# List products of the first four units, six pipeline steps later in the program

## The chip, the cores and the metric

One Trainium2 chip, one of its cores. The metric is the device time of one execution in microseconds (us). Before the change it is 1176.56 us, the median of 3 runs (1169.21 to 1182.27).

## What is computed

A depthwise causal convolution of seven taps over 8 x 2880 tokens of 192 channels, then a mixture of experts with one expert of 16 for each token. The reference, cut to what matters:

```python
out = np.einsum('hk,bskhg->bshg', softmax(weight), x_unf)      # 8 heads, 7 taps
x = out.reshape(23040, 192)
g_idx = np.argmax(x @ w_group, axis=1)                         # 4 groups
for g in range(4):
    xg = x[g_idx == g]
    e_idx = np.argmax(xg @ w_expert[g], axis=1)                # 4 experts of the group
    for e in range(4):
        h = np.maximum(xg[e_idx == e] @ w1[g, e], 0.0)         # 192 -> 1024
        out[tokens] = (g_w * e_w)[:, None] * (h @ w2[g, e])    # 1024 -> 192
```

## The kernel before

The 23040 tokens are cut into 192 blocks of 120 tokens, and these into 18 units: unit 0 has 4 blocks, unit 1 has 8, unit 2 has 12, units 3, 4 and 5 have 8, all others 12. `unit(u)` (line 392) is a generator. Each `yield` in it ends a step. Its steps are, in order: the load of the unit's x; eight convolution products, one for each head (line 416), each with its copy out of PSUM on ScalarE (lines 421 and 423); transposes of the result (lines 434 and 445); the router's logits (lines 459 and 464); the routing on VectorE (lines 495 to 524); the write of the convolved rows and gates to a table in memory (`xcd`, lines 425 and 528); the position of each token in its expert's list, from two small products with the running counts (lines 535 and 536) and a chain on VectorE (lines 539 to 572); and last the list product (line 577), which turns two one-hot matrices (`ohl`, line 564, and `ohv`, line 563) into a piece of each expert's token list, which VectorE finishes (lines 580 and 581) and GpSimd scatters into `idtab` (line 583). `finished(u)` then marks the unit as routed.

`step()` advances one live unit by one step, in rotation. Up to four units are live at first (`LIVE1`), and a new one is taken in when the newest has done a set number of steps (`SK`, 8 or 9). The main program calls `step()` until unit 4 is routed (`NEED` is 5). In that loop, at fixed counts of calls (`KPRE`: 40, 100, 112, 120, 126, 138), it also starts the weights of the first two experts and splits those of the first (`weights`, `split_one`, lines 613 to 629). A copy of such a split on ScalarE is pinned to its place in the program's order (`pin`). Then it opens the first two slots: the lists are read back (`open_portion`, line 975, on SP's queue) and the tokens' rows are gathered (`gather`, line 648, on GpSimd's queue). After that it makes another 72 calls (`AHEAD`), and then the expert phase begins: 256 tokens a slot, turned (line 661), hidden layer (line 679), output layer (line 697 and 701), scatter (line 752). The remaining units are spread over the slots at a rate which `stages_to` works out.

The written order is not each engine's order. A planner in the framework orders each engine's queue by when it expects an instruction's inputs; of several that are ready by its reckoning, the one that stands earlier in the program goes first. Once built, each engine takes its own queue in order.

Between the chain on VectorE and the list product stand some empty steps: `LISTLAG`, 8, from unit 5 on, and `LISTLAG0`, none, for units 0 to 4.

Of the kernel before, what the change touches and what calls it, by code (L numbers as in the profile page):

```python
# [35 lines left out]
def conv_moe_kernel(  # L36
# [56 lines left out]
    NEED = 5  # L93
# [12 lines left out]
    QGB = 3  # L106
    AHEAD = 72
    LISTLAG = 8
    LISTLAG0 = 0
    HOLD = 4  # L110
    LAG_S = 1
    HB = 4
# [17 lines left out]
    FRU = 99  # L130
    FRE = nc.gpsimd
    FRH = 0
# [254 lines left out]
    def gaps(u):  # L387

        return tuple(UG[4 * u:4 * u + 4]) if 4 * u < len(UG) else (GA, GL, GB, REST)


    def unit(u, pre=None):
# [177 lines left out]
        nc.vector.tensor_tensor(out=rows[:, 0:E], in0=eo, in1=sel, op=ALU.mult)  # L570
        nc.vector.tensor_reduce(out=rows[:, E:E + 1], in_=rows[:, 0:E], axis=AX.X, op=ALU.add)
        nc.vector.tensor_tensor(out=rowi, in0=rows[:, E:E + 1], in1=goff, op=ALU.add)
        for _ in range(LISTLAG if u >= NEED else LISTLAG0 if u < NEED - 1 else 0):
            yield
        pl = bank("l")
        for b in range(nb):
# [319 lines left out]

    def stages(u):
        q = units[u][1] // QB
        return 1 + 8 + (2 * FRH if u >= FRU else 0) + sum(gaps(u)) + 3 * q + 1 + (LISTLAG if u >= NEED else 0)

    SKEW1 = 8
    LIVE1 = 4
# [4 lines left out]
    def stages_to(n):  # L907
        extra = sum(max(0, stages(n) - i * SKEW2) for i in range(1, LIVE2)) if n < NU else 0
        return sum(stages(u) for u in range(n)) + extra
# [7 lines left out]
    def step():  # L917

        if routed[0] < NU and len(live) < lead[1] and (not live or max(live, key=lambda a: a[0])[1] >= (lead[0] or SK[min(routed[0], len(SK)) - 1])):
            u = routed[0]  # L920
            live.append([u, 0, unit(u, xin0 if u == 0 else None)])
            routed[0] += 1
        if not live:
            return
        done[0] += 1
        cur = live.pop(0)
        cur[1] += 1
        try:
            next(cur[2])
            live.append(cur)  # L930
        except StopIteration:
            pass
# [122 lines left out]
    while routed[1] < portions[0][0]:  # L1055
# [3 lines left out]
        for i in [i for i, kk in enumerate(KPRE) if kk == k]:  # L1059
            e, q = divmod(i, 5)  # L1060
# [162 lines left out]
```

## Time and profile before

| | us |
|---|---|
| median of 3 runs | 1176.56 |
| lowest and highest run | 1169.21, 1182.27 |
| profiled execution, its time | 1175.41 |
| profiled execution, its span | 1173.3 |
| TensorE busy in the span | 1115.3 |
| VectorE busy | 805.5 |
| ScalarE busy | 672.9 |
| first product of the expert phase | 102.85 after the span's start |

The profile is of one execution, whose time lies 2.1 us above its span and 1.15 us under the median. Busy time counts an engine as busy also where TensorE's clock is granted at its lower level, so a stretch can be full and slow at once. The granted clock stands in a column of its own, 1.00 for 2.4 GHz and 0.50 for 1.2 GHz, as a mean over the stretch.

### The profile page before, as it was taken

The numbers are of one execution on the slowest core, as the hardware profiler recorded it, in microseconds if no ns is written. First come the engines' busy times: TensorE is split into PE (matmuls) and PEld (weight loads), VectorE is DVE, ScalarE is ACT, GpSimd is POOL, SyncE is SP. The second block draws the span as 40 slices with busy tenths as digits, with TensorE's granted clock in tenths as the row PEclk, the third lists the DMA queues.
The fourth block names the chain that finished last, engine by engine and source line by source line (L and its number), as shares of the span: only waits on it lengthen the run. The fifth ranks groups of instructions, "written<-read, shape, count | busy, mean of one in ns | idle before, by whom it ended". The sixth has DMA issues, their size and how long they took to land. (4 is left out here: it accounts for less than half of the span.)

```text
span 1173.3 us, 23973 instructions
## 1 busy us (share of the span) xinstructions
PE 1115.3 (95%) x8468; PEld 1082.8 (92%) x8468; DVE 805.5 (69%) x1667; ACT 672.9 (57%) x1326; POOL 480.8 (41%) x432
## 2 busy tenths in 40 slices
PE   6799899999899999999999999999999999999993
PEld 6678899999899999999999999999999999999993
DVE  3757978886777676575678665666676767776671
ACT  4554566665565555646544555555676666766651
POOL 1002422345334343434435444444455655655541
PEclk9887899999899999999999999999999999999997
DMA  7989588979795564436454556444666667766630
GB/s 210 250 171 247 142 221 229 217 195 248 185 235 142 137 171 138 135 102 159 118 151 120 138 86 169 142 130 135 186 176 185 172 192 205 205 175 182 179 96 14
DMA packets 194093, 196.20 MB, mean 167 GB/s; under 512 B 49443, under 2 KB 171181, under 8 KB 193966
## 3 DMA queue, kind: packets, MB, share of 16 engines
q1 hardware_dynamic: 127424, 140.43, 45.0%
q0 software_dynamic: 18528, 36.09, 11.0%
q10 hardware_dynamic: 48014, 18.10, 7.4%
q8 instruction: 67, 1.10, 0.4%
q14 instruction: 60, 0.49, 0.2%
HBM read 159.08 MB, written 36.85 MB: 167 GB/s over the span
## 5 line engine op out<-in xcount | busy, mean ns | idle before, releaser
L697 PE MATMUL po<-cw,hh 128*128 128x384 f32 x1424 | 447.2, 371 | 11.7 <-DVE ys L749 9.4
L679 PE MATMUL ph<-xa,ah 128*128 128x256 f32 x1424 | 389.7, 295 | 0.7 <-DVE xa L664 0.7
L685 DVE SCALAR_TENSOR_TENSOR hl<-ph,hh 128x512 fp32r<-128x512 f32 x356 | 241.5, 686 | 174.0 <-ACT hh L684 173.6
L701 PE MATMUL po<-cw,hl 128*128 128x192 f32 x1424 | 358.3, 252 | 0.6 <-issue 0.3
L752 POOL DMA_INDIRECT out<-ys,idp x160 | 171.3, 1071 | 432.0 <-DVE ys L749 361.2
L684 ACT ACTIVATE hh<-ph 128x512 fp32r<-128x512 f32 x356 | 210.4, 595 | 231.4 <-PE ph L679 210.1
L697 PEld LDWEIGHTS po<-cw,hh 128*128 128x128 f32 x1424 | 269.7, 189 | 17.2 <-DVE ys L749 12.0
L701 PEld LDWEIGHTS po<-cw,hl 128*128 128x128 f32 x1424 | 273.8, 192 | 2.9 <-DVE hl L685 0.5
L679 PEld LDWEIGHTS ph<-xa,ah 128*128 128x128 f32 x1424 | 272.8, 192 | 3.1 <-DVE xa L664 1.0
L648 POOL DMA_INDIRECT xg<-xcd,idp x160 | 182.7, 1142 | 59.8 <-issue 27.1
L679 PE MATMUL ph<-xb,bl 128*128 128x256 f32 x712 | 202.1, 284 | 1.1 <-DVE bl L622 1.1
L679 PE MATMUL ph<-xa,al 128*128 128x256 f32 x712 | 202.2, 284 | 0.0
L679 PE MATMUL ph<-xb,bh 128*128 128x256 f32 x712 | 202.1, 284 | 0.0
L629 DVE TENSOR_TENSOR cw<-raw,cw 128x768 fp32r<-128x768 f32 x132 | 130.9, 1019 | 16.3 <-ACT cw L628 16.1
L679 PEld LDWEIGHTS ph<-xa,al 128*128 128x128 f32 x712 | 137.4, 193 | 1.8
L679 PEld LDWEIGHTS ph<-xb,bl 128*128 128x128 f32 x712 | 137.0, 192 | 1.3 <-DVE bl L622 1.3
L679 PEld LDWEIGHTS ph<-xb,bh 128*128 128x128 f32 x712 | 136.5, 192 | 0.0
L628 ACT ACTIVATE cw<-raw 128x768 fp32r<-128x768 f32 x132 | 105.4, 840 | 0.1
L614 DVE TENSOR_TENSOR al<-raw,ah 128x1024 fp32r<-128x1024 f32 x66 | 81.3, 1232 | 32.7 <-ACT ah L613 31.9
L749 DVE SCALAR_TENSOR_TENSOR ys<-po,xg,ys 128x192 f32<-128x192 f32 x187 | 75.7, 415 | 31.5 <-ACT ys L748 26.6
L667 ACT ACTIVATE xb<-pm 64x256 fp32r<-64x256 f32 (+1 forms) x98 | 36.1, 368 | 105.5 <-DVE xa L664 105.1
L748 ACT ACTIVATE ys<-po,xg 128x192 f32<-128x192 f32 x187 | 75.7, 418 | 28.7 <-PE po L701 14.0
(222 smaller groups left out, 1484.4 us busy)
## 6 DMA issues: line engine op xcount, KB each, us to landing
raw<-in_moe_w SPq DMA_DIRECT2D x132, 384.0 KB
raw<-in_moe_w SPq DMA_DIRECT2D x66, 512.0 KB
raw<-in_moe_w SPq DMA_DIRECT2D x132, 256.0 KB
xcd<-xc ACTq DMA_DIRECT2D x13, 742.5 KB
xin<-in_x SPq DMA_DIRECT2D x7, 1134.0 KB
xin<-in_x SPq DMA_DIRECT2D x6, 1039.5 KB
xcd<-xcb ACTq DMA_DIRECT2D x13, 360.0 KB
xg<-xcd,idp POOLq DMA_INDIRECT x160
```

The costliest lines, as they stand in the source:

```text
L614: eng.get(k, nc.vector).tensor_tensor(out=al, in0=ra, in1=ah.bitcast(F32), op=ALU.subtract)
L628: pin(PINW, nc.scalar.activation(out=cw[:, fs, 0, :], in_=rc[k - 2], func=AF.Copy))
L629: eng.get(k, nc.vector).tensor_tensor(out=cw[:, fs, 1, :], in0=rc[k - 2], in1=cw[:, fs, 0, :].bitcast(F32), op=ALU.subtract,)
L648: nc.gpsimd.indirect_dma_start(out=xs[:, t, :], out_offset=None, in_=xcd[0:known, :], in_offset=bass.IndirectOffsetOnAxis(ap=ids[:, t:t + ...
L679: nc.tensor.matmul(out=hp[:, j], lhsT=wgt[:, fs], rhs=xx, start=i == 0, stop=i == len(ops) - 1)
L684: nc.scalar.activation(out=hh, in_=hp, func=AF.Relu)
L685: nc.vector.scalar_tensor_tensor(out=hl, in0=hp, scalar=0.0, in1=hh.bitcast(F32), op0=ALU.max, op1=ALU.subtract,)
L697: nc.tensor.matmul(out=oo[t][:, 0:2 * D], lhsT=hh[:, j, ts], rhs=cw[:, f].rearrange("p a d -> p (a d)"), start=f == 0, stop=False,)
L701: nc.tensor.matmul(out=oo[t][:, 0:D], lhsT=hl[:, j, ts], rhs=cw[:, f, 0, :], start=False, stop=f == NF - 1,)
L748: nc.scalar.activation(out=ys[:, t, :], in_=oo[t][:, D:2 * D], func=AF.Copy, scale=g)
L749: nc.vector.scalar_tensor_tensor(out=ys[:, t, :], in0=oo[t][:, 0:D], scalar=g, in1=ys[:, t, :], op0=ALU.mult, op1=ALU.add,)
L752: nc.gpsimd.indirect_dma_start(out=outviews[nscat[0] % len(outviews)], out_offset=bass.IndirectOffsetOnAxis(ap=ids[:, t:t + 1].bitcast(U32 ...
```

## The change

```diff
-    LISTLAG0 = 0
+    LISTLAG0 = (6, 6, 6, 6, 0)
...
         nc.vector.tensor_tensor(out=rowi, in0=rows[:, E:E + 1], in1=goff, op=ALU.add)
-        for _ in range(LISTLAG if u >= NEED else LISTLAG0 if u < NEED - 1 else 0):
+        for _ in range(LISTLAG0[u] if u < NEED else LISTLAG):
             yield
         pl = bank("l")
...
     def stages(u):
         q = units[u][1] // QB
-        return 1 + 8 + (2 * FRH if u >= FRU else 0) + sum(gaps(u)) + 3 * q + 1 + (LISTLAG if u >= NEED else 0)
+        return 1 + 8 + (2 * FRH if u >= FRU else 0) + sum(gaps(u)) + 3 * q + 1 + (LISTLAG if u >= NEED else LISTLAG0[u])
```

Units 0 to 3 get six empty steps between the chain on VectorE and the list product with what follows it (two operations on VectorE, one scatter on GpSimd's queue). Unit 4 and the later ones keep what they had. The count of steps that sets the units' rate includes the new steps. No operation is added, taken away or changed in size.

## Rows read from the trace of the kernel before

**Rows 1.** The profile page, busy time of TensorE with its share of the span and its instructions, and the share of TensorE in 40 slices of the span, with the clock granted to it.
```profile
PE 1115.3 (95%) x8468; PEld 1082.8 (92%) x8468; DVE 805.5 (69%) x1667; ACT 672.9 (57%) x1326; POOL 480.8 (41%) x432
...
PE   6799899999899999999999999999999999999993
...
PEclk9887899999899999999999999999999999999997
```

**Rows 2.** Busy time by stretches (from:to in us, length, then busy us and instructions of each engine, TensorE's granted clock, share of the DMA engines, GB/s).
```profile
28.00:52.50 24.50, 21.69 (x166) 19.67 (x164) 18.58 (x82) 15.16 (x45) 2.12 (x2) 0.93 0.98 261
52.50:57.00 4.50, 0.05 (x3) 0.15 (x3) 4.47 (x14) 0.44 (x2) 0.00 (x0) 0.82 0.76 185
57.00:66.50 9.50, 9.50 (x53) 8.16 (x53) 4.14 (x16) 2.89 (x7) 0.96 (x1) 0.55 0.89 225
66.50:79.00 12.50, 9.72 (x78) 7.78 (x77) 10.07 (x46) 6.25 (x17) 0.95 (x1) 1.00 0.86 168
79.00:97.00 18.00, 16.79 (x115) 14.15 (x114) 9.13 (x32) 12.12 (x29) 6.82 (x7) 0.89 0.86 198
97.00:110.50 13.50, 12.27 (x58) 11.41 (x59) 9.86 (x32) 4.07 (x10) 2.87 (x3) 0.52 1.07 250
350.00:600.00 250.00, 248.07 (x1958) 244.06 (x1958) 168.11 (x341) 138.01 (x272) 99.60 (x90) 1.00 0.52 137
...
40.00:50.00 10.00, 9.00 (x64) 8.29 (x63) 9.08 (x33) 6.08 (x17) 0.99 (x1) 0.83 0.93 251
```

**Rows 3.** TensorE in order of time: start us, us, line, operation, idle time before it and what ended it. The list products of units 0 to 4 (line 577), the small products of units 0 and 4 (line 535), the first turn and the first product of the expert phase.
```profile
28.36 0.18 PE L535 MATMUL ph<-cum,tri 120*128 120x16 bf16 x1
...
31.91 0.25 PE L577 MATMUL po<-ohv,ohl 120*128 120x32 f16 x4 [1.32 <-DVE ohv L563]
...
43.05 0.35 PE L577 MATMUL ph<-ohv,ohl 120*128 120x32 f16 x8 [0.87 <-DVE ohv L563]
...
56.95 0.48 PE L577 MATMUL po<-ohv,ohl 120*128 120x32 f16 x12 [4.50 <-DVE ohv L563]
...
69.70 0.35 PE L577 MATMUL ph<-ohv,ohl 120*128 120x32 f16 x8 [0.50 <-DVE ohv L563]
...
74.04 0.19 PE L535 MATMUL pm<-cum,tri 120*128 120x16 bf16 x1
...
78.61 0.35 PE L577 MATMUL ph<-ohv,ohl 120*128 120x32 f16 x8 [2.23 <-DVE ohv L563]
...
97.00 0.45 PE L661 MATMUL pm<-ident,xg 128*128 128x128 f32 x1 [1.21 <-DMA xg<-xcd,idp]
...
102.85 0.56 PE L679 MATMUL ph<-xa,ah 128*128 128x256 f32 x1
```

**Rows 4.** TensorE in order of time, same columns: what stood in its queue behind the list product of unit 2 (the last convolution product of unit 5, the first and the last logits of unit 4), and a pair of logits rows in a stretch at full clock.
```profile
40.11 0.31 PE L459 MATMUL po<-wr,tb 128*120 128x40 f32 x2
40.25 0.57 PE L464 MATMUL po<-wr,ta 128*120 128x20 f32 x4
...
57.27 0.97 PE L416 MATMUL po<-xin,band 126*120 126x192 f32 x2
58.03 0.53 PE L459 MATMUL po<-wr,tb 128*120 128x40 f32 x2
58.36 0.97 PE L464 MATMUL po<-wr,ta 128*120 128x20 f32 x4
...
61.96 0.97 PE L464 MATMUL po<-wr,ta 128*120 128x20 f32 x4
```

**Rows 5.** VectorE in order of time, same columns: the splits of the first expert's weights (lines 614, 622, 629), unit 2's chain from its first to its last operation before the list product, the end of its list, and the start of unit 4's routing.
```profile
46.43 1.22 DVE L614 TENSOR_TENSOR al<-raw,ah 128x1024 fp32r<-128x1024 f32 x1
...
49.71 1.22 DVE L622 TENSOR_TENSOR bl<-raw,bh 128x1024 fp32r<-128x1024 f32 x1
50.91 0.17 DVE L539 TENSOR_TENSOR off<-pm,eoff 128x16 f32<-128x16 f32 x1
...
54.71 0.95 DVE L629 TENSOR_TENSOR cw<-raw,cw 128x768 fp32r<-128x768 f32 x1
...
56.34 0.56 DVE L563 TENSOR_TENSOR ohv<-ohr,idl 120x384 f16<-120x384 bf16 x1
...
57.69 0.19 DVE L581 SCALAR_TENSOR_TENSOR lsi<-po,none 128x32 int32<-128x32 f32 x1
62.96 0.33 DVE L495 TENSOR_REDUCE mx<-po 120x40 f32<-120x160 f32 x1 [5.08 <-PE po L464]
...
64.64 0.95 DVE L629 TENSOR_TENSOR cw<-raw,cw 128x768 fp32r<-128x768 f32 x1
```

**Rows 6.** GpSimd's queue in order of time: the list scatters of units 2, 3 and 4 and the first gather.
```profile
58.16 0.96 POOL L583 DMA_INDIRECT idtab<-lsi,rowi  x1 [12.66 <-DVE lsi L581]
70.78 0.95 POOL L583 DMA_INDIRECT idtab<-lsi,rowi  x1 [11.66 <-DVE xc L524]
79.69 0.96 POOL L583 DMA_INDIRECT idtab<-lsi,rowi  x1 [7.96 <-DVE lsi L581]
89.61 1.04 POOL L648 DMA_INDIRECT xg<-xcd,idp  x1 [8.96 <-DMA idp<-idtab]
```

**Rows 7.** SP's queue in order of time: the read of the lists.
```profile
83.10 0.39 SPq L975 DMA_DIRECT2D idp<-idtab  x1
```

**Rows 8.** ScalarE in order of time: the pinned copies of the first expert's splits, and a copy out of PSUM that waited for a transfer.
```profile
44.25 1.05 ACT L613 ACTIVATE ah<-raw 128x1024 fp32r<-128x1024 f32 x1
...
47.92 1.06 ACT L621 ACTIVATE bh<-raw 128x1024 fp32r<-128x1024 f32 x1
...
55.51 0.41 ACT L421 ACTIVATE xc<-ph 120x288 f32<-120x288 f32 x1 [2.98 <-DMA xcd<-xc]
```

## The prediction

> **What bounds the kernel now.** I read the page first, then the stretches, then the queues of the start one by one. TensorE is busy 95% of the span [rows 1], and in the middle of the expert phase it is busy 248.07 of 250 us at full clock (the stretch from 350, [rows 2]). There the work itself is the bound, and the change adds and removes none of it. Time can only be won or lost where TensorE waits or runs at its lower clock, and the slices show such a place at the start: the granted clock is 0.8, 0.8 and 0.7 in slices 2 to 4, about 29 to 117 us [rows 1].
>
> The stretches show how it looks there [rows 2]. From 52.5 to 57 TensorE does nothing while VectorE is busy 4.47 of 4.50 us. In the next 9.5 us TensorE is full, but at a granted clock of 0.55, mostly 1.2 GHz instead of 2.4. From 97 to 110.5 the clock is 0.52.
>
> The rows in order of time name the waits [rows 3]. All five list products of the start wait for `ohv`: 1.32, 0.87, 4.50, 0.50 and 2.23 us for units 0 to 4. Behind that of unit 2 stood work that did not need it, the last convolution of unit 5 and unit 4's logits [rows 4]. The late logits in turn held VectorE: it sat 5.08 us idle until 62.96, when unit 4's routing could begin [rows 5]. Unit 4 matters because its list ends the first stage: list product at 78.61, scatter at 79.69, read of the lists at 83.10, first gather at 89.61, first turn at 97.00, first expert product at 102.85 [rows 3, 6, 7].
>
> **The change, part by part.** One new step is one more call of `step()` for its unit, and with four units live three others move in between. So each list product goes some 24 calls behind its chain. Counting the generators as they are written, unit 0's product goes from call 56 to 80, unit 1's from 90 to 120, unit 2's from 133 to 169, unit 3's from 155 to 194, and unit 4's from 186 to 204. The two operations on VectorE and the scatter go with each. No instruction is new, so the cost lies in order alone. I take the pieces in turn.
>
> *The waits of units 0 to 3.* They sum to 1.32 + 0.87 + 4.50 + 0.50 = 7.2 us [rows 3]. In the new order unit 2's product (call 169) stands behind unit 5's last convolution (156) and unit 4's logits (151 and 155). The logits are four pairs of rows; a pair takes 0.31 + 0.57 less overlap, about 0.6 us at full clock by the starts 40.11 and the like, so 2.4 us, and with convolution and transposes there is enough work to cover most of 4.5 us. The bounds are 0 (the planner puts the products where they were) and 7.2; I take 7.2, since the inputs of what now stands in front are there (the logits followed at once when the product was out of the way, [rows 4]).
>
> *The clock behind those waits.* From 57 to 66.5, work that ran at 0.55 would have taken 9.5 x 0.45 = 4.3 us less, and from 40 to 50, at 0.83, 1.7 us less [rows 2]. The clock dropped around TensorE's waits there. If these go, up to 6.0 us come back; bounds 0 and 6.0, I take 6.0. With the waits this is 13.2 us.
>
> *Unit 4's tail.* Its own product keeps lag 0. From its small product at 74.04 to the list product at 78.61 are 4.57 us, of which TensorE waited 2.23 [rows 3]. More units live means units 6 and 7 enter later: at the end of the first loop they have done 9 and 0 steps instead of 12 and 3. So less work of theirs is at hand to fill this gap. The wait can grow by 4.57 - 2.23 = 2.3 us; bounds 0 and 2.3, I take 2.3 given back.
>
> *The gather.* From unit 4's list product to the first turn are 97.00 - 78.61 = 18.4 us [rows 3], a chain of scatter, read and gather that the change doesn't shorten. TensorE covered it with 16.79 us of work from 79 to 97, at a clock of 0.89 [rows 2]. At full clock that is 18 x 0.11 = 2.0 us less, and six steps' worth of unit work (24 of the 205 calls are empty, 181 against 187) falls behind the 72 calls: a unit's first logits and two transposes, some 1.8 us. Then 13.0 us of work stand against 18.4, a wait of 5.4 where 1.7 are idle now (the difference of 18.4 and 16.79, about): 3.7 us given back. Bounds 0 (the planner fills it with later units' work) and 3.7; I take 3.7. The slow clock behind it, 97 to 110.5, I leave as it is. The Trainium skill (DMA: Bandwidth & Descriptors, Anatomy of one DMA) gives a transfer a fixed cost of about 2 us; the hop from the scatter at 79.69 to the read at 83.10 took 3.4 us here, and by the page's figure this chain would be 1.4 us shorter and the gain 1.4 us larger, an estimate that I don't use.
>
> *The moved operations on VectorE and GpSimd.* `none` and `lsi` take about 0.19 us each (`lsi` did, [rows 5]), and the scatter 0.96 [rows 6]. Those of units 0 to 3 are read only when unit 4's list is there. Unit 3's now stands 10 calls before unit 4's, where 8.9 us lay between the scatters; they still go in order. A scatter took at most 3.4 us to let the read go, so I cost this at nothing, and at 3.4 if unit 3's were last.
>
> *The splits.* Their calls stay at 100, 112, 126 and 138 while the units' work moves some 12 calls later around them. So 1.22 + 1.22 + 0.95 + 0.95 = 4.3 us of VectorE [rows 5] and their pinned copies on ScalarE [rows 8] come sooner against unit 2's and unit 3's chains. VectorE is 9.08 of 10 us busy from 40 to 50 [rows 2], so these chains will be later; that was fatal when TensorE stood behind them, and the new distance covers it. I take nothing; the other end is the second rival.
>
> *The rest.* The unit rate of the expert phase goes up by about 2% for ten slots, as six steps are left over; I cost that at nothing, because TensorE's work is the same.
>
> The sum is 7.2 + 6.0 - 2.3 - 3.7 = 7.2 us. Against the profiled execution, 1175.41 - 7.2 = 1168.2; it lay 1.15 us under the median, so for the median 1176.56 - 7.2 = 1169.4 us.
>
> **The rivals.**
>
> *Nothing comes of it.* The written order is only a preference: unit 0's list product is written right behind its small products, and the trace has 3.5 us between them, 28.36 to 31.91, with other work in it [rows 3]. The planner may have counted those products as late already, and the time that is won before unit 4's list goes into the wait for the gather. For it: the wait of 5.08 us on VectorE is only one link, and unit 4's chain keeps its length. Against: unit 2's product did hold others that were ready. Time 1176.6, give or take 3.
>
> *The splits get in the way (slower).* The place is VectorE and ScalarE between 42 and 57 us. If the 4.3 us of splits push unit 2's and 3's chains, and through them unit 4's routing, TensorE waits 4.3 us more and pays the clock once more, 4.3 us as from 57 to 66.5: 1176.56 + 8.6 = 1185.2. It decides if unit 4's routing starts later than the 62.96 us of now. Against it: VectorE is idle 5.08 us just before. For it: a pinned copy whose weights have not landed would hold all that follows on ScalarE, as the copy at 55.51 did for 2.98 us [rows 8]. The Trainium skill (TensorE: Matmul & The Clock Gate, Architectural detail) has it that ScalarE and VectorE take their queues strictly in order. By that rule the whole of such a wait is paid by the PSUM copies behind it, and this rival keeps its chance; the trace agrees, since no copy passed the one at 55.51.
>
> *More than I count.* All 13.2 us come, nothing is given back, and the slow clock from 97 to 110.5 (13.5 x 0.48 = 6.5 us, [rows 2]) goes as well since TensorE meets the expert phase without a break: 1176.56 - 19.7 = 1156.9. Against it: the chain of 18.4 us.
>
> **How the numbers follow.** The forecast has 0.50, nothing 0.20, the splits 0.15, more 0.15. The likeliest is 1169.4; its own range, from half the 13.2 us given back and a little more to all of it kept, is 1163 to 1174. For 8 in 10 I leave out about half of each outer rival: 1159 to 1184. A change of 1%, 11.8 us, is about what a measurement of this kernel tells from none. Faster by more than that needs less than 1164.8: the third rival and a piece of the forecast, 0.22. Slower needs more than 1188.3, which the second rival reaches only if its price is half as large again: 0.08. Within 1%: 0.70.
>
> **What would show it.** Right, if the list products of units 0 to 3 wait together under 1 us, if unit 4's logits end before 57 us and its routing starts there, if the stretch from 57 to 66 has a clock near 1.00, and if the first expert product starts some 5 to 9 us before 102.85. Wrong in the sum, if that product comes early but the idle time before the first turn grows past 5 us; wrong in the mechanism, if unit 2's product still waits for `ohv`; and the second rival, if the splits stand in front of unit 2's chain on VectorE and TensorE waits for something else there.

## The result, and the profile after

The changed kernel takes 1183.38 us (median of 20 runs, 1174.11 to 1192.27), the kernel before 1174.59 us beside it (20 runs, 1168.97 to 1187.93). The ratio of the means, without the one slow run of either kernel, is 1.0062, with a 95% interval of 1.0036 to 1.0087 (the medians alone give 1.0075): slower by 4 to 10 us, where 7.2 us less were forecast. On a second chip it is 1.0095 (1.0062 to 1.0128; run e11 below). The profiled execution took 1187.38 us with a span of 1185.4, 12.1 more than the span before.

The page, the rows that answer to [rows 1]: the busy time of TensorE is the same 1115.3 us, so the work is unchanged; the slices at the start differ.

```profile
PE 1115.3 (94%) x8468; PEld 1082.9 (91%) x8468; DVE 803.8 (68%) x1667; ACT 670.5 (57%) x1326; POOL 485.1 (41%) x432
...
PE   6876989999899999999999999999999999999993
...
PEclk9877999999899999999999999999999999999997
```

The stretches, with the columns of [rows 2]:

```profile
28.00:52.50 24.50, 22.07 (x188) 20.55 (x188) 19.00 (x77) 13.08 (x40) 2.09 (x2) 0.98 0.94 224
52.50:57.00 4.50, 4.43 (x21) 3.91 (x21) 3.02 (x13) 3.14 (x11) 0.00 (x0) 0.50 1.05 214
57.00:66.50 9.50, 6.03 (x35) 4.86 (x34) 5.24 (x26) 0.00 (x0) 0.96 (x1) 0.50 1.03 294
66.50:79.00 12.50, 10.00 (x58) 7.59 (x58) 6.18 (x30) 4.70 (x14) 0.96 (x1) 0.78 0.65 124
79.00:97.00 18.00, 14.37 (x104) 11.96 (x104) 11.59 (x39) 13.24 (x35) 3.67 (x3) 1.00 0.91 212
97.00:110.50 13.50, 7.23 (x36) 6.81 (x36) 3.66 (x13) 1.46 (x4) 6.61 (x7) 0.59 1.08 285
110.50:160.00 49.50, 44.69 (x357) 43.15 (x358) 42.86 (x115) 25.34 (x48) 11.89 (x11) 0.94 0.57 145
```

For each stretch add the idle time to the busy time times one less the clock. From 28 to 79 that was 2.8 + 1.5, 4.5, 4.3 and 2.8, together 15.9 us before; now it is 2.4 + 0.4, 0.1 + 2.2, 3.5 + 3.0 and 2.5 + 2.2, together 16.3. The hole of 4.5 us ahead of 57 is full, but at 1.2 GHz, and the next two stretches lose what it gave. From 79 to 97, before 1.2 + 1.9 = 3.1 us were lost, now 3.6 + 0.0; from 97 to 110.5, before 1.2 + 5.9 = 7.1, now 6.3 + 3.0 = 9.3. From 110.5 to 160 it is 7.0 before and 7.5 now, by the row above and this one of before:

```profile
110.50:160.00 49.50, 45.75 (x368) 43.68 (x367) 42.70 (x107) 27.11 (x53) 16.98 (x15) 0.93 0.70 179
```

So from 28 to 160 us the two profiled executions differ by 3.6 us only. Another 2 us lie ahead of 28 us, and most of the rest behind 160; both come up again below.

TensorE in order of time, answering to [rows 3, 4]:

```profile
36.24 0.25 PE L577 MATMUL po<-ohv,ohl 120*128 120x32 f16 x4
...
45.06 0.35 PE L577 MATMUL ph<-ohv,ohl 120*128 120x32 f16 x8
...
57.33 0.97 PE L464 MATMUL po<-wr,ta 128*120 128x20 f32 x4
59.49 1.32 PE L416 MATMUL ph<-xin,band 126*120 126x288 f32 x2 [1.19 <-DMA xin<-in_x]
...
63.69 0.53 PE L577 MATMUL po<-ohv,ohl 120*128 120x32 f16 x12
68.09 1.31 PE L416 MATMUL pm<-xin,band 126*120 126x288 f32 x2 [3.87 <-ACT ta L436]
...
74.60 0.35 PE L577 MATMUL ph<-ohv,ohl 120*128 120x32 f16 x8
...
80.47 0.35 PE L577 MATMUL ph<-ohv,ohl 120*128 120x32 f16 x8 [2.38 <-DVE ohv L563]
...
103.27 0.45 PE L661 MATMUL pm<-ident,xg 128*128 128x128 f32 x1 [7.96 <-DMA xg<-xcd,idp]
...
113.96 0.56 PE L679 MATMUL ph<-xa,ah 128*128 128x256 f32 x1
```

The list products of units 0 to 3 wait for nothing now. Yet unit 4's comes at 80.47 instead of 78.61, the first turn waits 7.96 us for its gather, and the first expert product starts at 113.96 instead of 102.85. Why unit 4 isn't earlier stands on VectorE (in order of time, answering to [rows 5]):

```profile
58.71 0.55 DVE L563 TENSOR_TENSOR ohv<-ohr,idl 120x384 f16<-120x384 bf16 x1
...
61.70 0.17 DVE L539 TENSOR_TENSOR off<-pm,eoff 128x16 f32<-128x16 f32 x1 [2.34 <-PE pm L536]
...
64.25 0.19 DVE L580 TENSOR_SCALAR none<-po 128x32 f32<-128x32 f32 x1 [1.92 <-PE po L577]
...
64.51 0.18 DVE L581 SCALAR_TENSOR_TENSOR lsi<-po,none 128x32 int32<-128x32 f32 x1
...
64.81 0.32 DVE L495 TENSOR_REDUCE mx<-po 120x40 f32<-120x160 f32 x1
```

Unit 4's logits were done at 58.30 (57.33 + 0.97), 4.6 us earlier than before. But VectorE had `off`, `none` and `lsi` in front of their first reduction, and waited 2.34 and 1.92 us for TensorE's products of units 3 and 2. Unit 4's routing starts at 64.81, 1.85 us later than the 62.96 of before, and its list is 1.86 us later. The wait that left TensorE's queue came back in VectorE's. Run e3 below has the routing start at 57.94, ahead of `none`, and its next operation waits there all the same:

```profile
57.94 0.32 DVE L495 TENSOR_REDUCE mx<-po 120x40 f32<-120x160 f32 x1
64.43 0.19 DVE L580 TENSOR_SCALAR none<-po 128x32 f32<-128x32 f32 x1 [6.17 <-PE po L577]
...
65.23 0.31 DVE L496 TENSOR_TENSOR dd<-po,mx 120x160 f32<-120x160 f32 x1
```

There unit 4's list product came at 80.16, as late as in the changed kernel.

ScalarE and its queue, answering to [rows 8], where the same kind of wait was 2.98 us:

```profile
52.10 0.32 ACTq L528 DMA_DIRECT2D xcd<-xc  x1
...
67.02 0.41 ACT L421 ACTIVATE xc<-ph 120x288 f32<-120x288 f32 x1 [11.38 <-DMA xcd<-xc]
```

ScalarE stands still from 55.64 to 67.02, until unit 2's row write (742.5 KB, the same in all kernels), issued at 52.10, has left the buffer that unit 6's first copy needs; TensorE's wait of 3.87 us at 68.09 is behind that.

GpSimd's queue and SP's read of the lists, answering to [rows 6, 7]:

```profile
77.01 0.96 POOL L583 DMA_INDIRECT idtab<-lsi,rowi  x1 [11.09 <-DVE eold L544]
84.18 0.96 POOL L583 DMA_INDIRECT idtab<-lsi,rowi  x1 [6.21 <-DMA xcd<-xcb]
...
86.84 0.39 SPq L975 DMA_DIRECT2D idp<-idtab  x1
...
93.98 2.10 POOL L648 DMA_INDIRECT xg<-xcd,idp  x1 [8.85 <-DMA idp<-idtab]
```

Unit 4's list was ready on VectorE at 81.38; its scatter went at 84.18, 7.2 us after unit 3's. Before it went 0.28 us after the list (79.41, 79.69), and unit 3's lay 8.9 us back. The profile ends the idle time of 6.21 us with another transfer (`xcd<-xcb`), and with other names in other runs. VectorE shows what it was: its next `rowi` (line 572, with the row numbers of a list; two buffers in rotation) waited for a list scatter until 83.51, when only unit 3's can have been under way, and unit 4's scatter followed 0.67 us later.

```profile
83.51 0.16 DVE L572 TENSOR_TENSOR rowi<-rows,goff 128x1 int32<-128x1 f32 x1 [1.09 <-DMA idtab<-lsi,rowi]
```

The same wait of `rowi` stands 0.67 to 0.74 us ahead of the late scatter in e1, e2, e5, e6, e8 to e11, e13, e15 and e18.

### The profile page after: what moved, and what is told of

Its sections match the earlier page's. It is cut to its first block, busy times and chain, and to the rows that moved or that the text cites. A ratio compares the mean times of both kernels' runs of the same rounds, so it can differ in the third digit from the quotient of the medians.

```text
span 1185.4 us, 23968 instructions
## 1 busy us (share of the span) xinstructions
PE 1115.3 (94%) x8468; PEld 1082.9 (91%) x8468; DVE 803.8 (68%) x1667; ACT 670.5 (57%) x1326; POOL 485.1 (41%) x432
## 6 DMA issues: line engine op xcount, KB each, us to landing
xcd<-xc ACTq DMA_DIRECT2D x13, 742.5 KB
```

## The experiments

Five sets; the kernels of a set shared a chip and their runs of the kernel before, and each ratio is to these. Experts are counted from 0; the turn is TensorE's transposing of the first gathered rows (line 661), and calls are those of `step()`. Theories on record: A, the order of SP's loads and the write that holds ScalarE; B, the late list products and their scatters; C, the splits; D, the first turn stands too early. In TensorE's queue as built, 34 first halves of logits (line 459) stand ahead of the first turn before, and 30 after the change: the empty steps use up calls, so six steps less are done when the turn comes.

**Set 1: loads and write (A, C).** e1 starts expert 1's weights 12 calls later, behind unit 6's x; e2 moves all such calls by about as much as the units' work; e3 issues the early units' row write on GpSimd's queue; e4 gives the kernel before the crossed order of loads.

```diff
-    KPRE = [40, 100, 112, 126, 138, 120]
+    KPRE = [40, 100, 112, 126, 138, 132]    (e1, on the changed kernel)
+    KPRE = [40, 108, 124, 138, 151, 132]    (e2, on the changed kernel)
+    KPRE = [40, 100, 112, 126, 138, 111]    (e4, on the kernel before)
```

```diff
-                SE.dma_start(out=xcw[:, :, 0:WB], in_=xc[0:BT, 0:nb])
+                (nc.gpsimd if u < NEED else SE).dma_start(out=xcw[:, :, 0:WB], in_=xc[0:BT, 0:nb])    (e3, changed)
```

> The changed kernel with one number different: the weights of expert 1 are started at call 132 instead of 120, so that they stand behind unit 6's x on SP's queue again, as they did before the change. Theory A (the weights passed unit 6's x, the bunched loads held up unit 2's row write, and ScalarE stood 11.4 us on it): ScalarE's wait for that write falls under 4 us, unit 4's list product comes before 76 us, the first expert product before 104 us, time 0.995 to 1.001 of before. Rival B (the late list products themselves: unit 3's scatter holds unit 4's): the hold on ScalarE may go but the first expert product stays at 110 us or later, time 1.004 to 1.009. Rival C (the splits of expert 0, which come earlier against the units): nothing changes against the changed kernel, 1.006.

> The changed kernel with all calls of the weights and of the splits moved to where they stood against the units' steps before the change (100 to 108, 112 to 124, 126 to 138, 138 to 151, 120 to 132). Theory A: as with the weights moved alone, within 0.003 of it. Rival C: clearly better than with the weights moved alone, which stays at 1.006, and at or under 1.000 itself. Rival B: 1.004 to 1.009.

> The changed kernel with the row writes of units 0 to 4 (line 528) issued from GpSimd's queue instead of ScalarE's; the weights of expert 1 still stand ahead of unit 6's x. Theory A with the place of the write in ScalarE's queue as the main part: the write is issued at about 50 instead of 52.1 us and ahead of the loads, ScalarE's wait falls under 6 us, time 0.998 to 1.003. Theory A with the bunched loads as the main part: the write still lands after 62 us, ScalarE waits more than 8 us, time 1.004 to 1.008. Rivals B and C: as the changed kernel, about 1.006, whatever ScalarE's wait does.

> The kernel before, list products undelayed, with one number different: the weights of expert 1 are started at call 111 instead of 120, ahead of unit 6's x (call 112). Theory A: the order of the loads alone does the harm, so ScalarE waits more than 6 us for unit 2's row write (2.98 before) and the time is 1.003 to 1.009 of before. Rivals B and C: within 0.002 of before, with ScalarE's wait near 3 us.

Measured: e1 1.0038 (1.0003 to 1.0073), e2 1.0031 (0.9998 to 1.0063), e3 1.0105 (1.0060 to 1.0150), e4 1.0008 (0.9982 to 1.0034). e1 put unit 6's x ahead again, but ScalarE still stood 10.9 us. e2 halved that wait (5.6 us), and the turn still waited 7.8. In e3 unit 2's write went out at 50.80 and the copy that needs its buffer came at 62.59, ScalarE was held 7.5 us, and its ratio is the highest of all, outside of what any theory expected. e4 is the telling one: in the kernel before ScalarE was held 6.9 us and unit 4's list came at 82.62, later than in the changed kernel, and the time did not move. So a hold of 6.9 us and a late fourth list need not cost anything. (The crossed order is not shown to make that hold: e7 below, whose order up to the opening is that of the kernel before, has 6.3 us of it, and e17 none.) Splits that move with the work (e2) may save some 3 us, not the whole, and the interval of e2 overlaps that of the changed kernel; C as the main cause isn't borne out.

**Set 2: the number of calls ahead of the expert phase (D).**

```diff
-    AHEAD = 72
+    AHEAD = 78       (e5, on the changed kernel)
+    AHEAD = 90       (e8, on the changed kernel)
+    AHEAD = 66       (e7, on the kernel before)
```

```diff
-    LISTLAG0 = (6, 6, 6, 6, 0)
+    LISTLAG0 = (0, 0, 6, 0, 0)       (e6, on the changed kernel)
```

> The changed kernel with 78 calls between the opening of the first slots and the first turn instead of 72, which gives back the six steps of unit work that the empty steps displaced. In TensorE's queue 34 instead of 30 pairs of line 459 then stand ahead of the first turn, as in the kernel before. Theory D (the changed kernel's loss is the first turn, which stands in TensorE's queue ahead of logits that used to cover the gather): the wait at the first turn falls from 8.0 to under 6 us, the first expert product comes before 110 us, time 0.997 to 1.003 of before. Theory A (loads and ScalarE's hold before unit 4's list) and rival B (scatters in a row): nothing changes against the changed kernel, 1.006, first expert product near 114 us.

> The kernel before with the six empty steps for unit 2 alone, whose list product held TensorE 4.50 us; unit 6's x stays ahead of the weights of expert 1. TensorE's first turn stands at the same place of its queue as in the changed kernel, 30 pairs of line 459 ahead of it. Theory D: a wait of 5 us or more at the first turn, 1.002 to 1.007 of before, though unit 4's list product comes before 76 us. Theory A: 0.993 to 1.000, since the loads keep their order. Rival B: 0.995 to 1.000, since unit 3's list product isn't late.

> The kernel before, list products undelayed, with 66 calls instead of 72 ahead of the first turn, so that 30 instead of 34 pairs of line 459 stand ahead of it, as in the changed kernel. Theory D: TensorE waits 4 to 8 us at the first turn, the first expert product comes at 106 to 112 us, 1.003 to 1.008 of before, with no list product moved. Theories A and B: within 0.002 of before.

> The changed kernel with 90 calls instead of 72 ahead of the first turn; all 36 pairs of line 459 of the start stand ahead of it in TensorE's queue. Theory D: the wait at the first turn is under 3 us, the first expert product comes near 106 us, 0.993 to 1.000 of before. Theories A and B: 1.004 to 1.009.

Measured: e5 0.9972 (0.9939 to 1.0006), e8 0.9973 (0.9942 to 1.0004), e7 1.0013 (0.9983 to 1.0042), e6 0.9990 (0.9962 to 1.0019). With 78 calls the turn is behind 34 again, and the changed kernel is no longer slower, though ScalarE is held 11.2 us as before. But taking six calls from the kernel before (e7) costs hardly anything, though its first expert product comes at 109.55, and e6, where the turn stands behind 30 as well, is not slower either: its turn waits 0.28 us where D expected 5 or more. D holds for the changed kernel and missed twice. e5's VectorE shows the same as the changed kernel's: unit 4's routing follows unit 2's `lsi` at once.

```profile
60.93 0.18 DVE L581 SCALAR_TENSOR_TENSOR lsi<-po,none 128x32 int32<-128x32 f32 x1
61.23 0.32 DVE L495 TENSOR_REDUCE mx<-po 120x40 f32<-120x160 f32 x1
```

**Set 3: what makes the write late (A').** In the changed kernel the loads of expert 2's weights start at 51.33, where they started at 55.68, and unit 2's write lands after some 14.9 us, where it took 6.5. e9 keeps those loads behind the read of the lists; e10 adds the six calls; e12 is the control on the kernel before; e11 is the changed kernel unaltered.

```diff
-    NPIN = (0, 0)
+    NPIN = (2, 3)        (e9, e10 on the changed kernel; e12 on the kernel before)
-    AHEAD = 72
+    AHEAD = 78           (e10 as well)
```

> The changed kernel once more, so that the next ones stand beside it on one chip. All theories expect about 1.006 of the kernel before, by the first measurement (1.0036 to 1.0087), a first turn that waits about 8 us for its gather, and the first expert product at about 114 us.

> The changed kernel with the weights of expert 2 kept in program order on SP's queue, so that their big loads stand behind the read of the lists instead of ahead of it; no other engine's order changes. Theory A' (unit 2's row write lands late, 14.9 us after its issue, because these loads start at 50.5 to 53.5 us already and crowd it): the write lands in under 10 us, ScalarE's copy of unit 6 waits under 6 us instead of 11.4, and TensorE loses at least 4 us less from 52 to 80. Theory D (the first turn stands ahead of the work that used to cover the gather): the first turn still waits 7 to 9 us, and the time stays at 1.002 to 1.006 of the kernel before, since what is won before the fourth list is waited out at the turn. If A' is the whole cause: within 0.002 of the kernel before, or under it.

> As the last one, and 78 calls after the opening of the first two slots instead of 72, which puts back the six steps that the empty ones took out of the stretch behind the opening. A' and D together: the turn waits under 2 us for its gather, ScalarE's copy under 6 us, first expert product at 100 to 106 us, and the time is 0.993 to 0.997 of the kernel before, less than that of the changed kernel with 78 calls alone. D alone: 0.996 to 0.999, as with 78 calls alone.

> The kernel before with the weights of expert 2 kept in program order in the same way, as a control: if the hold by itself is worth something or costs something at expert 2's first slot. A' expects ScalarE's wait of 2.98 us to shrink and the time within 0.002 of the kernel before, since the fourth list and the turn are not late there; D the same. A time of over 1.003 would mean that late weights of expert 2 cost something, and the two others are to be read less that.

Measured: e11 1.0095 (1.0062 to 1.0128), e9 1.0045 (1.0009 to 1.0080), e10 0.9983 (0.9949 to 1.0017), e12 1.0050 (1.0027 to 1.0072). A' missed in e9: ScalarE was held 8.35 us, not under 6; unit 2's write, issued at 52.64, held until 64.53, 11.9 us instead of 14.9. The hold of the loads costs the kernel before 0.5%. From e9 to e10 only the calls differ: 1178.80 to 1171.12 us. TensorE in e9, then in e10:

```profile
101.71 0.45 PE L661 MATMUL pm<-ident,xg 128*128 128x128 f32 x1 [9.17 <-DMA xg<-xcd,idp]
...
112.29 0.56 PE L679 MATMUL ph<-xa,ah 128*128 128x256 f32 x1
```

```profile
100.36 0.45 PE L661 MATMUL pm<-ident,xg 128*128 128x128 f32 x1 [5.03 <-DMA xg<-xcd,idp]
...
104.96 0.56 PE L679 MATMUL ph<-xa,ah 128*128 128x256 f32 x1
```

The turn is hardly earlier, but with four more of the logits' first halves in front of it instead of behind it the expert phase starts 7.3 us sooner: the time fell by 7.7. The unaltered program, e11, is a warning on reading one execution. Its profiled one was the quickest of its six (1177.88 us):

```profile
79.58 0.37 PE L577 MATMUL ph<-ohv,ohl 120*128 120x32 f16 x8 [2.38 <-DVE ohv L563]
...
97.24 0.33 PE L661 MATMUL pm<-ident,xg 128*128 128x128 f32 x1 [1.48 <-DVE endr L545]
...
105.61 0.56 PE L679 MATMUL ph<-xa,ah 128*128 128x256 f32 x1
```

There the first gather, at 89.25, followed the read of the lists, issued at 85.63, by 3.6 us and not by 7.1, and the turn waited 1.48 us. The wait of 8 us is in the profiles of the changed kernel, e1, e2, e3 and e9, and not in each execution.

**Set 4: empty steps without moved products (B against D).** e13 makes the six empty steps behind the list product and scatter: the queue has the turn behind 30, as in the changed kernel, and every product stands in its old place within its unit. e14 leaves unit 3 out of the change, e15 does unit 3 alone, e16 is e14 with 78 calls.

```diff
-        for _ in range(LISTLAG0[u] if u < NEED else LISTLAG):
+        for _ in range(0 if u < NEED else LISTLAG):
             yield
         pl = bank("l")
...
         finished(u)
+        for _ in range(LISTLAG0[u] if u < NEED else 0):
+            yield                                     (e13)
```

```diff
-    LISTLAG0 = (6, 6, 6, 6, 0)
+    LISTLAG0 = (6, 6, 6, 0, 0)       (e14; e16 with AHEAD = 78)
+    LISTLAG0 = (0, 0, 0, 6, 0)       (e15)
```

> The six empty steps of units 0 to 3 stand behind the list product and its scatter instead of ahead of them: no product is moved in its unit, but the units live as long as in the changed kernel, and in TensorE's queue the first turn stands behind 30 of the logits' first halves as there, not behind 34 as before. Theory D (what costs is the place of the turn): the first turn waits 3 to 8 us for its gather, the first expert product starts after 107 us, and the time is 1.003 to 1.008 of the kernel before. Theory B (what costs is the late list products and scatters): the scatter of unit 4 is issued within 1.5 us of its list as before, the turn waits under 3 us, and the time is within 0.002 of the kernel before.

> The change without its part for unit 3 (six steps for units 0, 1 and 2 alone). The turn stands behind 30 of the logits' first halves, as in the changed kernel, but unit 3's scatter leaves TensorE's and GpSimd's way earlier. Theory B: unit 4's scatter is issued within 1.5 us of its list instead of 2.6, the stretch from unit 4's list product to the first turn is 18 to 20 us instead of 22.8, and the time is 1.000 to 1.004 of the kernel before. Theory D alone: the turn still waits over 5 us and the time is 1.004 to 1.008.

> The part of the change for unit 3 alone. Here the turn keeps its place behind 34 of the logits' first halves, as before. Theory B: unit 4's scatter waits for unit 3's as in the changed kernel (issued over 2 us behind its list), the turn comes 2 to 3 us later, and the time is 1.002 to 1.005 of the kernel before. Theory D: what the scatter costs is covered by the work ahead of the turn, which waits under 3 us, and the time is within 0.002 of the kernel before.

> Six steps for units 0, 1 and 2 alone, and 78 calls instead of 72, which puts the turn back behind 34 of the logits' first halves. Theory D: the turn waits under 3 us, the first expert product starts by 106 us, and the time is 0.004 or more below that of the run with 72 calls beside it, 0.994 to 0.999 of the kernel before. Theory B alone: within 0.002 of the run with 72 calls.

Measured: e13 1.0044 (1.0013 to 1.0075), e14 1.0017 (0.9992 to 1.0043), e15 1.0026 (0.9994 to 1.0057), e16 0.9953 (0.9924 to 0.9983). The empty steps alone cost 5 us with no product moved. How, is not as D had it. TensorE in e13, and its stretch from 79 to 97:

```profile
74.56 0.36 PE L577 MATMUL ph<-ohv,ohl 120*128 120x32 f16 x8
...
82.94 0.85 PE L416 MATMUL ph<-xin,band 126*120 126x288 f32 x2 [3.77 <-DMA xin<-in_x]
...
101.27 0.33 PE L661 MATMUL pm<-ident,xg 128*128 128x128 f32 x1 [0.19 <-DVE endr L545]
...
108.27 0.56 PE L679 MATMUL ph<-xa,ah 128*128 128x256 f32 x1
```

```profile
79.00:97.00 18.00, 14.23 (x58) 12.01 (x57) 4.13 (x11) 6.85 (x14) 6.06 (x6) 0.62 0.92 209
```

Unit 4's list is 4 us early (of units 6 and 7 less stands in front of it, by the counts of calls), but then TensorE runs into an x that hasn't landed, and goes on at a mean clock of 0.62 to a turn whose gather started at 89.18, about when it did before. The turn waits for next to nothing here, where D expected 3 to 8 us; and unit 4's scatter went 2.4 us after its list with no product moved, where B expected under 1.5.

e14 missed D in the same way: its turn does not wait for its gather, and the stretch ahead of it has the low clock too.

```profile
99.03 0.33 PE L661 MATMUL pm<-ident,xg 128*128 128x128 f32 x1 [0.51 <-DVE mx L541]
```

```profile
79.00:97.00 18.00, 15.68 (x67) 13.04 (x66) 5.57 (x15) 6.79 (x16) 5.58 (x6) 0.62 0.81 191
```

In e15 the turn stands behind 34 and still waits, as unit 4's scatter (list ready at 83.25) had to let unit 3's pass. GpSimd's queue and TensorE in e15:

```profile
78.00 0.96 POOL L583 DMA_INDIRECT idtab<-lsi,rowi  x1 [15.37 <-DVE lsi L581]
85.11 0.96 POOL L583 DMA_INDIRECT idtab<-lsi,rowi  x1 [6.15 <-DVE pick L520]
...
102.86 0.45 PE L661 MATMUL pm<-ident,xg 128*128 128x128 f32 x1 [5.65 <-DMA xg<-xcd,idp]
```

So B's step is real; its time of 1.0026 is not told from none. e14 to e16 differs in the calls alone, and went from 1183.12 to 1174.82 us, intervals apart: 8 us again. But neither turn waits for its gather, and up to 160 us the two profiled executions lose the same, 39.3 and 39.8 us of idle time and clock, against 40.3 and 36.2 behind it. So where e16 wins isn't shown. e16 is faster than the kernel before, by some 5.5 us.

**Set 5: calls or products?** e17 is the kernel before with 78 calls, e18 is e13 with 78 calls.

```diff
-    AHEAD = 72
+    AHEAD = 78       (e17 on the kernel before, e18 on e13)
```

> The kernel before with 78 calls instead of 72: the list products stay where they were, and the first turn stands behind 36 of the logits' first halves instead of 34. If the six more calls are worth something by themselves, whatever the list products do: 0.993 to 0.998 of the kernel before. If they only put back what the empty steps took (theory D), the turn of the kernel before is covered already, and the time is within 0.002 of it.

> The empty steps behind the list products, as in the run with the empty steps alone, and 78 calls: every list product in its old place, and the turn back behind 34 of the logits' first halves. Theory D: within 0.002 of the kernel before, as both sides of the change are undone, and what the changed kernel with 78 calls gains over this one is what the moved list products are worth, 0.003 to 0.005. If the gain of 0.003 to 0.005 is here as well, it is not the list products' but that of the calls.

Measured: e17 1.0027 (0.9994 to 1.0060), e18 1.0047 (1.0022 to 1.0072). Six more calls give nothing where the list products stay; D as first put, that the calls undo the cost of the empty steps, falls with e18. Its TensorE meets a late x again (4.85 us at 90.39), and its turn, at 111.49, waits for nothing. Between e17 and e18, which differ in the empty steps alone, 0.0020 isn't told from none.

## Why the prediction was wrong

Put the runs in a square, each to the kernel before on its chip:

| | 72 calls, turn behind 30 | 78 calls, turn behind 34 |
|---|---|---|
| empty steps, products not moved | 1.0044 (e13) | 1.0047 (e18) |
| products of units 0 to 2 moved | 1.0017 (e14) | 0.9953 (e16) |
| products of units 0 to 3 moved | 1.0062, 1.0095 (changed kernel) | 0.9972 (e5) |

The prediction added 13.2 us won by the moved products and 6.0 given back, the most of it by the empty steps, as if each came by itself. The second is near in size: about 5 us (0.0044 and 0.0047), though only part of it by the cover that I named. The first depends on the column. With the turn back in its place the moved products are worth 1.0047 - 0.9972 = 0.0075 to 1.0047 - 0.9953 = 0.0094, 9 to 11 us against e18; against e17, the kernel before with the same calls, the change is worth 0.0055 to 0.0074 in all, 6 to 9 us. With the turn where the change puts it they are worth 3 us for three units, and cost 2 to 6 us for four; the intervals of that column overlap, so these last two aren't told from none. (Where the two terms of such a difference are from two chips, it is an estimate.)

A reading that fits the six times: two ways end at the first turn, TensorE's own queue and the chain list, scatter, read, gather. Moving the products shortens the first and leaves the second as it was, or longer; where the turn stands early in the queue, what TensorE wins is lost again ahead of the expert phase. The profiles bear this out for the changed kernel against e5, and for e9 against e10: up to 160 us, idle time and clock (in stretches of 4 us) lose 47.8 against 39.2 and 47.8 against 39.1, and the wait at the turn goes from 7.96 to none and from 9.17 to 5.03. They don't for e14 against e16, as said above. And e6, with the turn behind 30 and unit 2's product moved, is at 0.9990.

The term of the sum that failed is the 13.2 us. From 28 to 79 the changed kernel loses 0.4 us more than the kernel before, not 13.2 less. Of the 6.0 given back behind that, some 3 came (79 to 160).

By the prediction's own steps:

- *The waits of units 0 to 3*: right, 7.2 us of them are gone. But it asked only what stands behind the product on TensorE. What stands behind `none` and `lsi` on VectorE is unit 4's routing, and in the changed kernel, e5, e9 and e16 it starts 0.30 us after `lsi`. This step failed: the logits came 4.6 us sooner and the routing 1.85 us later. It is not the whole of it: in e6, e14 and e16, where unit 3's product is not delayed in its unit, the stretches from 28 to 79 lose 9.7, 9.8 and 9.6 us, so 6 us do come there. In e14 and e16 the routing also follows `lsi` at once, and unit 2's write took as long (14.1 and 13.8 us), but ScalarE came to the copy that needs it only at 64.27 and 64.56, not at 55.64, and was held 1.85 and 0.88 us, not 11.38. In e5, held 11.20 us, the same stretches lose 16.3. Which of the two holds, VectorE's or ScalarE's, makes the 6 us isn't separated.
- *The clock behind those waits*: wrong. From 57 to 66.5 it is 0.50, not near 1.00; TensorE waited 0.78 and 1.14 us ahead of 50.46 and 52.25 and was busy 4.43 of the next 4.50 us at 1.2 GHz. Waits and clock together lose 16.3 us from 28 to 79 against 15.9, instead of 13.2 less.
- *Unit 4's tail*: 2.3 us were given back by my sum, but the wait grew only by 0.15 (2.23 to 2.38).
- *The gather*: the sign was right, two sizes off. I held its chain at 18.4 us and the cover at 13.0. The chain took 22.8 us (80.47 to 103.27), with 2.8 us in the scatter and 1.9 more from gather to turn; the wait was 7.96, not 5.4. Six of the logits' first halves, with what belongs to them, then ran behind the turn, ahead of the first expert product, where it was two before.
- *The moved operations*: "at nothing, and at 3.4 if unit 3's were last" was the wrong choice of the two. Unit 4's scatter, 7.2 us behind unit 3's, went 2.8 us after its list in the changed kernel and 1.9 in e15; without unit 3's part it went 0.28 us after it in e14. But in e13 and e6, where unit 3's product was not moved in its unit, it was 2.4 and 3.3 us late as well.
- *The splits*: this rival gave 1185.2 us, near the 1183.38, and its condition was met (routing after 62.96), but for another reason, so that its number is near is luck: moving the splits back with the work (e2, 1.0031) isn't told from the changed kernel. ScalarE was held by a row write, 11.38 us, not by a pinned copy. The rule that the prediction took from the Trainium skill (TensorE: Matmul & The Clock Gate, Architectural detail), that ScalarE takes its queue strictly in order, was borne out: no copy passed the one that waited. VectorE did the same at 61.70 and 64.25.

What stays open: of the 12.1 us between the two profiled executions more than half lies behind 160 us. Idle time and clock in stretches of 4 us (20 us from 400 on) add up there to 35.9 us before and 43.3 after. The second profiled execution of the changed kernel (e11) has 39.4, and e17, where no product moved, 46.7; no run isolates it. The 2 us ahead of 28 us (11.2 against 9.2) are hardly the change's: e7 and e17, whose program is that of the kernel before up to there, lose 10.8 and 11.3. Nor is it settled why TensorE's clock fell at 52, or what the x of e13 and e18 came late behind. No run takes ScalarE's wait away without touching the loads or the order, as a further buffer for `xc` would.

## What to carry to other kernels

When a wait is taken out of one engine's queue, follow the same operation through the other in-order queues that it feeds: here the next consumer stood behind it on VectorE, and the stall changed engines. Gains ahead of a join count only if the queue that gained is the last to arrive; so find the other way into it (here the gather), and try moving the consumer back together with the work that covers it (0.9953 to 0.9983 here, though only part of how is shown). An empty step in a hand-written order isn't free: it shifts each later load and call against it, which cost 5 us in e13 with no product moved in its unit.

## What was not expected of the hardware

In thirteen profiles (the changed kernel, e1, e2, e5, e6, e8 to e11, e13, e15, e16 and e18) a scatter whose list had been ready for 1.9 to 3.3 us went 6.9 to 9.1 us after the one ahead of it; the `rowi` on VectorE that waits in front of such a scatter was released 6.2 to 8.4 us after the issue of the one ahead. The read of the lists went 2.3 to 6.1 us after its scatter. Unit 2's row write of 742.5 KB, the same in all kernels, was waited for until 6.5 us after its issue in the kernel before, 14.9 after the change and 10.9 in e4, with the DMA engines' share at 0.76 from 52.5 to 57 before and 1.05 after. The early loads may be one cause: with them held (e9, e10) it took 11.9 and 12.7 us, against 13.3 to 14.9 in the four profiles of the same order without (the changed kernel, e5, e8, e11). They are not the only one, and in the kernel before holding them (e12) didn't shorten it: 8.4 us, with 9.5 in e7.
